# Another order for the first two batches of a packed attention and gated FFN kernel

## The chip, the cores and the metric

One NeuronCore of a Trainium2 chip runs the whole program. The metric is the device time of one execution in microseconds. The engines are TensorE (PE, matmuls and transposes; PEld is its weight load), VectorE (DVE), ScalarE (ACT), GpSimd (POOL) and SyncE (SP), which issues every DMA of this kernel.

## The reference, cut to what matters

```python
def _attn_ref(q, k, v, p):                    # q, k, v: 8 x 8 x 576 x 64, p: 8 x 8 x 32 x 64
    def sm_attn(qq, kk, vv):
        s = scale * np.matmul(qq, kk.transpose(0, 1, 3, 2))
        a = softmax(s)
        return np.matmul(a, vv)
    p_packed = sm_attn(p, k, v)               # softmax 1: 32 rows over 576 keys
    return sm_attn(q, p_packed, p_packed)     # softmax 2: 576 rows over 32 keys

x = attn_out.transpose(0, 2, 1, 3).reshape(4608, 512)
out = ((x @ w_a) * (x @ w_b)) @ w_out         # w_a, w_b: 512 x 1536, w_out: 1536 x 512
```

All inputs and the output are float32.

## The kernel before, in words

**Tiling.** The kernel goes batch by batch (8 batches of 576 tokens). For a batch, stage1 computes the packed attention for the even and the odd heads (e = 0, 1): scores on PE, maximum on DVE, exponential on ACT, transposes of the result on PE with copies on ACT, product with v on PE. stage2 computes the second attention as far as its probabilities: scores on PE, a transpose and a maximum on DVE, the difference (L328) on DVE or POOL, the exponential (L330) on ACT, sum and reciprocal on DVE, the product with the reciprocal (L337) on the engine of the difference, a transpose back on DVE (L341), a cast to the high part a_hi on ACT (L347) and the low part a_lo on DVE. The weights are not multiplied with x: g_tiles (L371) multiplies the packed values with a 256-column piece of w_a and of w_b, giving g, split into ghi (ACT, L377) and glo (DVE); mm1 (L389) multiplies g with the probabilities. The two factors come in two halves pa and pb; ACT copies pa to asb (L401), DVE multiplies pb into it (L404), which frees the two pairs of PSUM banks, and ACT and POOL split the result h into h_hi (L408) and h_lo. mm2 (L415, later L724) multiplies h with the split w_out. Every product of two split numbers is three matmuls: high by high, high by low, low by high.

**Weight words.** The weights arrive as raw 64-bit words in 36 pieces of 512 KB: piece 4c + n, for c = 0 to 5, holds a quarter of column block c of w_a (n = 0, 1) or w_b (n = 2, 3), and pieces 24 to 35 are rows of w_out. A piece takes three steps: A, its high words on ACT (high_word, L194); B, its low words on ACT (L202), DVE or POOL (both L199), as the digit of the piece in WAYS says (0 ACT, 1 DVE, 2 POOL); C, the join on DVE (both_words, L205). A C frees the piece's buffer, and SP may then load a further piece; 12 buffers exist. For w_out a step D follows, which splits the joined f32 tile on ACT and POOL; that tile, wo_f, has one buffer. A_i, B_i, C_i stand for the steps of piece i, counted from 0.

**The order.** The order on every engine and in SP's queue is the order of emission; nothing is moved by a scheduler. FIRST loads p, k, q, v of batch 0 and the first 11 pieces. START is the order of batch 0 up to its first product: T turns p, k0 to k4 and q0 to q4 turn the five parts of k and q (PE transposes, then copies on DVE or ACT by a digit of TURN, first five digits k, 0 DVE, 1 ACT), S0, r0 (e = 0) and S1, r1 (e = 1) are the next steps of stage1, P turns the packed values, s0 and s1 are the next steps of stage2, W is filler (nine matmuls without use, L562), g the first g_tiles, Lp, Lv, Lk, Lq are loads of the next batch. PLAN_0 is the order during batch 0: 37 slots divided by bars, two in each of the 12 mm1 (after pa and after pb), then one after each step of mm2; its steps S, r, s, T, P, k, q, L belong to batch 1. g_tiles for mm1 4 and 5 stands before mm1 3, and so on in pairs. PLAN is the same for batch 1, with steps of batch 2. From batch 2 on, 72 periods (period) follow STEPS, repeated every 24, and FILLS gives the number of mm2 matmuls between their products. SUBS gives the engine of L328 and L337 for batch 0, e = 0 and 1, and batch 1, e = 0 and 1 (0 POOL, 1 DVE); later batches use POOL.

**Loads.** Eight DMAs are out at a time: the issue of one waits until the eighth before it has landed. A half of k of a batch is four DMAs of 144 KB in 128-byte rows (L116), and is turned by one DVE transpose (L124).

Of the kernel before, what the change touches and what calls it, by code (L numbers as in the profile page):

```python
# [19 lines left out]
def tile_packed_attn_gated_ffn(  # L20
# [175 lines left out]
    def low_word(raw, way):  # L196
        low = raw[..., 0]
        if way:
            (nc.vector if way == 1 else nc.gpsimd).tensor_scalar(  # L199
                out=low, in0=low, scalar1=2.0 ** -29, scalar2=7.0, op0=ALU.mult, op1=ALU.min)  # L200
        else:
            nc.scalar.activation(out=low, in_=low, func=AF.Copy, scale=0.93 * 2.0 ** -29)  # L202
# [107 lines left out]
    def stage2(b, e):  # L310
# [17 lines left out]
        eng.tensor_tensor(out=s2, in0=s2, in1=mx.unsqueeze(2).broadcast_to([P, TU, J]), op=ALU.subtract)  # L328
# [180 lines left out]
    PLAN_0 = ("A | C C | B A B A | B C C B C | A A | C | B | C B A T0 k0 Lp2 A | A A B B C Lq0 | C C k1 | A B A | "
# [127 lines left out]
    for b in range(NB):  # L637
        plan = dict(PLAN if b else PLAN_0)
        slot, tasks, late_steps = [0], {"g": next_g(b + 1)} if b == 0 else {}, [""]

        def between():

            steps, _, late_steps[0] = plan.get(slot[0], "").partition(";")
            if b == 0:
                emit(1, steps, tasks)
            else:
                if 2 <= slot[0] and slot[0] % 4 == 0 and kept[0] < NC:
                    keep_weights()
# [307 lines left out]
```

## Time and profile before

| | us |
|---|---|
| median of the runs (lowest, highest) | 715.92 (714.87, 716.61) |
| profiled execution, its own time | 714.0 |
| its span | 712.2 |
| busy: PE, DVE, POOL, ACT | 699.0, 449.8, 417.8, 363.2 |
| start of the first product of batch 0 (L389) | 34.68 |
| filler W before it (L562) | 7.99 |

A row of the order in time gives start, duration, engine, line, operation, tile written and tiles read, shape, count of merged instructions, and in brackets the idle time before it with what ended it. In a row of windows come the stretch, its length, busy time and instructions of PE, PEld, DVE, ACT and POOL, the granted PE clock, the share of the DMA engines and GB/s.

### The profile page before, as it was taken

How to read it: one execution, taken by the hardware profiler on the slowest of the kernel's cores; microseconds unless marked ns; L12 is line 12 of the kernel's file. 1: busy time of each engine (PE TensorE's matmuls, PEld its weight loads, DVE VectorE, ACT ScalarE, POOL GpSimd, SP SyncE). 2: the span in 40 equal slices, each digit the busy share in tenths (PEclk: the TensorE clock that was granted, in tenths of full speed). 3: DMA queues.
4: the chain of work that ended last, by engine and by line, in shares of the span. 5: the costliest groups of instructions: out<-in, count | busy, mean ns of one | idle time of the engine just before them, and what ended most of it. 6: DMA issues, size and time to landing. Idle time of an engine off the chain costs nothing.

```text
span 712.2 us, 14198 instructions
## 1 busy us (share of the span) xinstructions
PE 699.0 (98%) x5558; PEld 574.2 (81%) x5558; DVE 449.8 (63%) x819; ACT 363.2 (51%) x733; POOL 417.8 (59%) x322
## 2 busy tenths in 40 slices
PE   6899999999999999999999999999999999999998
PEld 4488877888778887887888788788888888888887
DVE  3888755367455669665875668765785657754342
ACT  3788753554344455644563456554554455544520
POOL 0496753337334687745874579566776578856520
PEclk9999999999999999999999999999999999999999
DMA  8999872767344735555453574457146323133002
GB/s 230 387 274 315 220 162 53 193 153 282 93 98 139 211 96 141 139 138 146 134 111 115 142 195 93 106 176 182 61 98 180 105 89 119 61 110 127 1 1 74
DMA packets 177059, 102.37 MB, mean 144 GB/s; under 512 B 141280, under 2 KB 159456, under 8 KB 171616
## 3 DMA queue, kind: packets, MB, share of 16 engines
q1 hardware_dynamic: 176992, 101.47, 50.3%
q8 instruction: 43, 0.70, 0.4%
q14 instruction: 24, 0.20, 0.1%
HBM read 85.72 MB, written 15.73 MB: 142 GB/s over the span
## 4 chain that ended last, share of the span: by engine, by line
PE 94%; DVE 2%; SPq 1%; DMA 1%; ACT 1%; issue 0%; DVEq 0%; ACTq 0%
PE x L724 37%; PE m L765 29%; PE m L389 9%; PE x L779 5%; PE m L415 5%; PE s L301 2%; PE s L316 1%; PE s L255 1%; PE x L371 1%; PE s L291 1%; SPq L116 1%; DMA kn<-in_k_dram 1%; DMA nat<-in_k_dram 0%; PE m L152 0%; PE x L152 0%
## 5 line engine op out<-in xcount | busy, mean ns | idle before, releaser
L724 PE MATMUL x<-wo,h_hi 128*128 128x512 f32 (+1 forms) x776 | 249.3, 391 | 0.0
L91 POOL TENSOR_TENSOR h_lo<-asb,h_hi 128x576 fp32r<-128x576 f32 x96 | 140.3, 1462 | 83.3 <-ACT h_hi L810 44.6
L724 PEld LDWEIGHTS x<-wo,h_hi 128*128 128x128 f32 x776 | 140.8, 188 | 22.2 <-ACT gs L785 1.0
L724 PE MATMUL x<-wo,h_lo 128*128 128x512 f32 (+1 forms) x388 | 152.1, 392 | 0.0
L91 POOL TENSOR_TENSOR G_lo<-gs,G_hi 128x640 fp32r<-128x640 f32 x72 | 113.0, 1575 | 30.6 <-ACT G_hi L800 30.3
L724 PEld LDWEIGHTS x<-wo,h_lo 128*128 128x128 f32 x388 | 72.9, 188 | 11.8
L91 POOL TENSOR_TENSOR A_lo<-gs,A_hi 128x256 fp32r<-128x256 f32 x36 | 27.2, 754 | 89.7 <-ACT A_hi L788 89.7
L847 DVE TENSOR_TENSOR d<-m,d 128x576 f32<-128x576 f32 (+1 forms) x73 | 54.0, 740 | 34.6 <-ACT d L843 33.8
L860 DVE TENSOR_TENSOR asb<-m,d 128x288 f32<-128x288 f32 x72 | 32.4, 451 | 66.4 <-ACT c L856 64.8
L856 ACT COPY c<-m 128x288 f32<-128x288 f32 x72 | 28.8, 399 | 78.6 <-PE m L765 78.6
L734 DVE TENSOR_TENSOR part<-x,part 128x512 f32<-128x512 f32 (+1 forms) x65 | 44.1, 678 | 38.8 <-PE x L724 38.8
L765 PE MATMUL m<-tx_hi,G_hi 128*128 128x288 f32 x216 | 63.8, 296 | 0.0
L765 PE MATMUL m<-tx_hi,G_lo 128*128 128x288 f32 x216 | 63.7, 295 | 0.0
L785 ACT COPY gs<-x 128x512 f32<-128x512 f32 x36 | 21.1, 587 | 82.8 <-PE x L779 81.2
L765 PE MATMUL m<-tx_lo,G_hi 128*128 128x288 f32 x216 | 63.3, 293 | 0.0
L800 ACT CAST G_hi<-gs 128x640 fp32r<-128x640 f32 x72 | 52.2, 730 | 15.1 <-POOL gs L794 14.5
L843 ACT COPY d<-m 128x576 f32<-128x576 f32 (+1 forms) x73 | 46.6, 639 | 20.2 <-PE m L765 18.6
L810 ACT CAST h_hi<-asb 128x576 fp32r<-128x576 f32 x72 | 49.0, 680 | 11.5 <-DVE asb L874 11.5
L765 PEld LDWEIGHTS m<-a_hi,G_hi 128*128 128x128 f32 x144 | 27.0, 187 | 31.6 <-issue 17.4
L794 POOL TENSOR_TENSOR gs<-gs 128x512 f32<-128x512 f32 x36 | 46.7, 1296 | 2.6 <-DVE gs L791 2.5
L765 PE MATMUL m<-a_hi,G_hi 128*128 128x288 f32 x144 | 47.0, 326 | 0.0
L389 PE MATMUL m<-a_hi,ghi 128*128 128x288 f32 x192 | 43.2, 307 | 1.5 <-ACT ghi L377 1.5
(171 smaller groups left out, 1548.7 us busy)
## 6 DMA issues: line engine op xcount, KB each, us to landing
wr<-w_kept SPq DMA_DIRECT2D x36, 1024.0 KB
nat<-in_k_dram SPq DMA_DIRECT2D x56, 144.0 KB
nat<-in_q_dram SPq DMA_DIRECT2D x56, 144.0 KB
vt<-in_v_dram SPq DMA_DIRECT2D x28, 256.0 KB
out_dram<-part SPq DMA_DIRECT2D x27, 256.0 KB
raw<-in_moe_w_a_dram SPq DMA_DIRECT2D x12, 512.0 KB
raw<-in_moe_w_b_dram SPq DMA_DIRECT2D x12, 512.0 KB
raw<-in_moe_w_out_dram SPq DMA_DIRECT2D x12, 512.0 KB
```

What stands on the lines that cost most here:

```text
L91: return eng.tensor_tensor(out=dst, in0=src, in1=hi.bitcast(F32), op=ALU.subtract)
L389: nc.tensor.matmul(out=ps[:, half, 0:HS], lhsT=gt[:, kt, ft % 4, cols], rhs=at[:, kt, HS * half:HS * half + HS], start=(n == 0 and kt == 0 ...
L415: nc.tensor.matmul(out=o[:, cols], lhsT=ht[:, c0:c0 + P], rhs=wt[:, cols], start=(ft == 0 and n == 0), stop=(ft == NFT - 1 and n == 2))
L724: nc.tensor.matmul(out=o[:, cols], lhsT=ht[:, c0:c0 + P], rhs=wt[:, cols], start=(ft == fts[0] and n == 0), stop=end)
L734: nc.vector.tensor_tensor(out=parts[i][:, cols], in0=o[:, cols], in1=parts[i][:, cols], op=ALU.add)
L765: nc.tensor.matmul(out=bank[:, n % 2, 0:HS], lhsT=g, rhs=t, start=(first and i == 0), stop=(i == 2), skip_group_check=True)
L779: nc.tensor.matmul(out=gps[e][J * r:J * r + J, :], lhsT=ppT[rows, 2 * (b % 2), r, :], rhs=w[rows, r, :], start=True, stop=True)
L794: nc.gpsimd.tensor_tensor(out=gs[:, 2:4].rearrange("p a u f -> p a (u f)"), in0=gs[:, 0:2].rearrange("p a u f -> p a (u f)"), in1=s2.unsqu ...
L800: nc.scalar.copy(out=G_hi[:, n % 3], in_=gs[:, 1:6, n % 2])
L810: nc.scalar.copy(out=view(h_hi[ft]), in_=src)
L843: nc.scalar.copy(out=d[:, both], in_=X[:, both, 0:HS])
L847: nc.vector.tensor_tensor(out=d[:, both], in0=V[:, both, 0:HS], in1=d[:, both], op=ALU.add)
```

## The change

Nothing but constants changes: the order strings START, PLAN_0, PLAN, STEPS and FILLS, and the engine strings WAYS, TURN and SUBS. The instructions of PE are the same ones. On SP, in START, the load of p of batch 1 moves ahead of piece 13, pieces 18 and 19 move ahead of v and k of batch 1, and the two halves of k follow each other with pieces 20 and 21 behind them (before: v, first half, pieces 18 to 20, second half, piece 21).

```diff
-    START = ("T0 k0 k4 k1 k3 k2 q0 S0 S1 r0 r1 q1 r1 r0 r0 r1 r0 q2 r1 q3 q4 P0 s0 B s1 W A s0 B A A s0 s0 B s1 C "
-             "A s1 B s0 C s1 A s1 C B B Lp2 C A B A s0 s1 B C B B s0 B g A C A A s1 Lv2 Lk2 C C A A C B B Lk3 C s1")
-    WAYS = ("000000022220202120012012011200010010")
-    TURN = ("0001110101")
-    SUBS = ("0100")
+    START = ("T0 k0 k1 k3 k2 k4 q0 S0 r0 r1 r1 q1 r1 r0 r0 S1 A q3 r0 r1 B q2 B q4 P0 C s0 s0 s1 A B A s0 B Lp2 A A s0 s1 B s1 C B s1 A A W C s0 C A s1 C B s0 s1 C s0 g A B B A s1 B A C C s1 Lv2 B Lk2 Lk3 B C C B A")
+    WAYS = ("220000002222201201112002111221210002")
+    TURN = ("1111110000")
+    SUBS = ("0011")
...
-    PLAN_0 = ("A | C C | B A B A | B C C B C | A A | C | B | C B A T0 k0 Lp2 A | A A B B C Lq0 | C C k1 | A B A | "
-              "S0 B | B A r0 | C C C | B A Lq1 |  | C C B r0 r0 D A A | S1 C D | B C B B A D | r1 C | A A D | r0 T2 "
-              "|  | q0 B r1 C B D r1 C |  | A | D B C Lv1 A r1 | A B D Lk2 B C B q1 D Lk3 A A P0 | C s0 s0 D C Lp4 "
-              "A B | s1 s0 | Lv2 | D | s0 s1 s0 | k2 s0 s1 C k3 | s1 |  | Lq2 D s0 s1 s1 Lq3 s1")
+    PLAN_0 = ("A A | C C | A B | C B C A B | B A | C | C B | A A B B C T0 k0 Lp2 A | Lq0 C | B k1 C | A A B | C S0 C B | A r0 | B A C B C | A | | B C r0 Lq1 C r0 D A | C A D B S1 | A B C D | B r1 C r1 | A B D | r0 T2 | | C r1 A B D | C A | q0 C | Lv1 B r1 A D | B B Lk2 q1 Lk3 A D A C P0 B | A C s0 s0 C A Lp4 D | D s1 | Lv2 D | s0 s1 B s0 | C s0 | k2 s1 D s1 | s1 | s0 k3 s0 | Lq2 Lq3 s1 s1")
```

PLAN is rewritten in the same way, with the steps of batch 2 at most two slots from their old places. In STEPS single steps move by one place within a period or to the next one, for instance `11: {... 'h': 'Lq2', 'c': 'u2 G'}` to `11: {... 'h': 'G Lq2', 'c': 'u2'}`. In FILLS two entries change by one: `(5, 0, 5)` to `(5, 1, 4)` and `((5, 4, 4), (6, 5, 0))` to `((5, 3, 4), (7, 5, 0))`.

More of the change, by code (lines that the diff above doesn't have):

```diff
@@ L499, in tile_packed_attn_gated_ffn @@
     FIRST = ("p0 k0 k2 k1 q0 v0 q1 v1 q2 w1 w1 w1 w1 w1 w1 w1 w1 w1 w1 w1")
-    START = ("T0 k0 k4 k1 k3 k2 q0 S0 S1 r0 r1 q1 r1 r0 r0 r1 r0 q2 r1 q3 q4 P0 s0 B s1 W A s0 B A A s0 s0 B s1 C "
-             "A s1 B s0 C s1 A s1 C B B Lp2 C A B A s0 s1 B C B B s0 B g A C A A s1 Lv2 Lk2 C C A A C B B Lk3 C s1")
-    WAYS = ("000000022220202120012012011200010010")
-    TURN = ("0001110101")
-    SUBS = ("0100")
-    PLAN = (" |  |  | S0 | r0 | r0 |  | r0 |  | r0 Lv1 ; S1 | r1 | r1 q0 Lk2 | r1 | r1 | q1 Lk3 Lv2 P0 |  ; s0 | s0 s0 | s0 T2 | "
-            "s0 Lp4 | s0 s1 | s1 s1 | s1 | s1 | s1 | t0 t1 t2 t3 u0 | k2 |  | k3 Lq2")
+    START = ("T0 k0 k1 k3 k2 k4 q0 S0 r0 r1 r1 q1 r1 r0 r0 S1 A q3 r0 r1 B q2 B q4 P0 C s0 s0 s1 A B A s0 B Lp2 A A s0 s1 B s1 C B s1 A A W C s0 C A s1 C B s0 s1 C s0 g A B B A s1 B A C C s1 Lv2 B Lk2 Lk3 B C C B A")
+    WAYS = ("220000002222201201112002111221210002")
+    TURN = ("1111110000")
+    SUBS = ("0011")
+    PLAN = ("| | | S0 | r0 | | r0 | r0 | | r0 ; Lv1 S1 | r1 r1 | q0 Lk2 | r1 | r1 q1 Lk3 | Lv2 P0 | ; s0 | s0 s0 | T2 Lp4 | s1 | | s1 s1 s0 | | s1 s0 s1 | s0 k2 s1 | t0 u0 t1 k3 | | | t2 Lq2 t3")
     PLAN = dict(enumerate(PLAN.split("|")))
-    PLAN_0 = ("A | C C | B A B A | B C C B C | A A | C | B | C B A T0 k0 Lp2 A | A A B B C Lq0 | C C k1 | A B A | "
[3 rows of a table removed]
+    PLAN_0 = ("A A | C C | A B | C B C A B | B A | C | C B | A A B B C T0 k0 Lp2 A | Lq0 C | B k1 C | A A B | C S0 C B | A r0 | B A C B C | A | | B C r0 Lq1 C r0 D A | C A D B S1 | A B C D | B r1 C r1 | A B D | r0 T2 | | C r1 A B D | C A | q0 C | Lv1 B r1 A D | B B Lk2 q1 Lk3 A D A C P0 B | A C s0 s0 C A Lp4 D | D s1 | Lv2 D | s0 s1 B s0 | C s0 | k2 s1 D s1 | s1 | s0 k3 s0 | Lq2 Lq3 s1 s1")
     PLAN_0 = dict(enumerate(PLAN_0.split("|")))
@@ L892, in tile_packed_attn_gated_ffn @@
         between()
-    STEPS = {-2: {'post': 'u1 u2', 'd': 'G', 'h': 'H', 'b': 'u3'}, -1: {'post': 'H', 'h': 'G'}, 0: {'pre': 'S0', 'a': 'r0', 'c': 'H Lq1', 'w': 'G Lv1', 'end': 'r0'}, 1: {'pre': 'G', 'a': 'H', 'b': 'r0 r0', 'w': 'r0'}, 2: {'post': 'S1 H', 'h': 'r1', 'c': 'G'}, 3: {'pre': 'G', 'd': 'r1', 'a': 'r1', 'b': 'r1 H', 'f': 'q0', 'end': 'r1'}, 4: {'v': 'H', 'h': 'G', 'b': 'Lk2'}, 5: {'pre': 'P0 q1', 'd': 'G', 'v': 'T2', 'end': 's0 H'}, 6: {'pre': 'Lv2', 'post': 'Lk3 Lp4', 'v': 'H', 'a': 's0', 'b': 'G', 'c': 's0'}, 7: {'pre': 's0', 'post': 'H', 'a': 's0 G', 'c': 's0', 'end': 's0'}, 8: {'pre': 's1', 'post': 's1', 'd': 'H', 'a': 's1', 'c': 'G s1'}, 9: {'pre': 'k2', 'post': 'G', 'd': 's1', 'a': 'H', 'h': 's1', 'f': 's1', 'end': 't0'}, 10: {'v': 't1 t2 t3', 'a': 'u0', 'b': 'G', 'end': 'H'}, 11: {'post': 'u1', 'v': 'H', 'a': 'k3', 'h': 'Lq2', 'c': 'u2 G', 'f': 'u3'}, 12: {'pre': 'S0', 'b': 'Lq1', 'w': 'G', 'f': 'Lv1', 'end': 'H'}, 13: {'pre': 'G r0', 'd': 'r0', 'v': 'H', 'h': 'r0', 'b': 'r0', 'w': 'r0'}, 14: {'post': 'S1', 'a': 'H', 'b': 'G'}, 15: {'pre': 'G', 'post': 'H r1', 'd': 'r1', 'a': 'r1', 'h': 'r1', 'f': 'q0', 'end': 'r1'}, 16: {'v': 'G', 'h': 'H', 'b': 'Lk2', 'end': 'P0 q1'}, 17: {'pre': 'G', 'a': 'T2', 'b': 'H', 'end': 's0'}, 18: {'post': 'Lv2 s0 Lk3', 'v': 'G', 'h': 'Lp4', 'b': 's0', 'c': 'H', 'f': 's0'}, 19: {'pre': 'G', 'post': 's0', 'b': 's0', 'end': 'H s0'}, 20: {'pre': 's1', 'd': 's1', 'a': 's1 H', 'c': 's1', 'w': 'G'}, 21: {'pre': 'k2 G', 'v': 's1', 'a': 'H', 'w': 's1', 'f': 's1', 'end': 't0 t1'}, 22: {'pre': 't2', 'v': 'u0 H', 'h': 'G'}, 23: {'pre': 'u1', 'v': 'G t3', 'a': 'H', 'h': 'k3', 'c': 'Lq2 u2', 'end': 'u3'}}
@@ new lines, in tile_packed_attn_gated_ffn @@
+    STEPS = {-2: {'post': 'u1 u2', 'd': 'G', 'h': 'H', 'b': 'u3'}, -1: {'h': 'H G'}, 0: {'pre': 'S0', 'a': 'H', 'c': 'Lq1', 'w': 'Lv1 r0', 'f': 'G'}, 1: {'pre': 'G', 'v': 'r0', 'a': 'H', 'b': 'r0 r0', 'w': 'r0'}, 2: {'post': 'S1 H', 'b': 'r1', 'c': 'G'}, 3: {'pre': 'G', 'd': 'r1', 'a': 'r1', 'h': 'H', 'b': 'r1', 'f': 'q0', 'end': 'r1'}, 4: {'pre': 'H', 'h': 'G', 'b': 'Lk2', 'c': 'P0'}, 5: {'post': 'G', 'd': 'q1', 'v': 'T2', 'end': 's0 H'}, 6: {'pre': 'Lv2', 'post': 'Lk3 Lp4', 'v': 'H', 'a': 's0', 'b': 'G', 'c': 's0'}, 7: {'pre': 's0', 'post': 'H', 'a': 's0 G', 'w': 's0', 'end': 's0'}, 8: {'pre': 's1', 'post': 's1', 'd': 'H', 'a': 's1', 'c': 'G s1'}, 9: {'pre': 'k2', 'post': 'G', 'd': 's1', 'a': 'H', 'h': 's1', 'f': 's1', 'end': 't0'}, 10: {'post': 't1', 'v': 't2 t3', 'a': 'u0', 'b': 'G', 'end': 'H'}, 11: {'post': 'u1', 'v': 'H', 'a': 'k3', 'h': 'G Lq2', 'c': 'u2', 'f': 'u3'}, 12: {'pre': 'S0', 'b': 'Lq1', 'c': 'Lv1', 'w': 'G', 'end': 'H'}, 13: {'pre': 'G r0', 'v': 'H r0', 'h': 'r0', 'b': 'r0', 'w': 'r0'}, 14: {'post': 'S1', 'v': 'H', 'b': 'G'}, 15: {'pre': 'G', 'post': 'H r1', 'd': 'r1', 'a': 'r1', 'h': 'r1', 'f': 'q0'}, 16: {'pre': 'r1', 'v': 'G', 'h': 'H', 'b': 'Lk2', 'c': 'P0', 'end': 'q1'}, 17: {'pre': 'G', 'a': 'T2', 'b': 'H', 'w': 's0'}, 18: {'post': 'Lv2 s0 Lk3', 'v': 'G', 'a': 'H', 'b': 'Lp4', 'f': 's0 s0'}, 19: {'pre': 'G', 'post': 's0', 'c': 's0', 'end': 's1 H s0'}, 20: {'a': 's1 H', 'h': 's1', 'w': 'G', 'f': 's1'}, 21: {'pre': 'k2 G', 'd': 's1', 'a': 'H', 'w': 's1', 'f': 's1', 'end': 't0 t1'}, 22: {'pre': 't2', 'v': 'u0', 'a': 'H', 'h': 'G', 'end': 't3'}, 23: {'pre': 'u1', 'a': 'G', 'h': 'H k3', 'c': 'Lq2 u2', 'end': 'u3'}}
@@ L894, in tile_packed_attn_gated_ffn @@
     banks_of["x"], banks_of["v"] = bank_pair(), bank_pair()
-    FILLS = [((5, 2, 5), (5, 7, 0)), ((11, 1, 8), (9, 7, 0)), ((5, 0, 5), (6, 8, 0)), ((4, 3, 3), (6, 8, 0)), ((4, 4, 4), (5, 7, 0)), ((6, 3, 3), (7, 5, 0)), ((5, 3, 2), (9, 5, 0)), ((4, 4, 4), (5, 7, 0)), ((5, 4, 4), (6, 5, 0)), ((9, 7, 5), (10, 5, 0)), ((4, 4, 4), (5, 7, 0)), ((9, 4, 7), (8, 8, 0))]
+    FILLS = [((5, 2, 5), (5, 7, 0)), ((11, 1, 8), (9, 7, 0)), ((5, 1, 4), (6, 8, 0)), ((4, 3, 3), (6, 8, 0)), ((4, 4, 4), (5, 7, 0)), ((6, 3, 3), (7, 5, 0)), ((5, 3, 2), (9, 5, 0)), ((4, 4, 4), (5, 7, 0)), ((5, 3, 4), (7, 5, 0)), ((9, 7, 5), (10, 5, 0)), ((4, 4, 4), (5, 7, 0)), ((9, 4, 7), (8, 8, 0))]
```

## The prediction

> **What bounds the kernel now.** I read the page, then the chain of waits, then the rows of each engine in order of time for the first 70 us, the stretch that the change reorders.
>
> ```profile
> PE 699.0 (98%) x5558; PEld 574.2 (81%) x5558; DVE 449.8 (63%) x819; ACT 363.2 (51%) x733; POOL 417.8 (59%) x322
> PE 94%; DVE 2%; SPq 1%; DMA 1%; ACT 1%; issue 0%; DVEq 0%; ACTq 0%
> ```
>
> TensorE is busy for 699.0 of 712.2 us and carries 94% of the chain. The change adds no matmul and takes none away, so it can win only holes in PE's row, or lose by making new ones. PE's rows in order of time (start, duration, instruction, idle time before it and its releaser) show where holes are:
>
> ```profile
> 23.46 7.99 PE L562 MATMUL m<-kn,ident 128*128 128x512 f32 x18
> 31.63 1.57 PE L371 MATMUL x<-w_ab,ppT 64*32 64x512 f32 x16 [0.17 <-DVE w_ab L205]
> 34.68 0.54 PE L389 MATMUL m<-a_hi,ghi 128*128 128x288 f32 x2 [1.48 <-ACT ghi L377]
> 37.27 0.54 PE L389 MATMUL m<-a_lo,ghi 128*128 128x288 f32 x2 [0.26 <-DVE a_lo L91]
> 38.80 1.18 PE L371 MATMUL x<-w_ab,ppT 64*32 64x512 f32 x16
> 44.91 0.43 PE L389 MATMUL m<-a_hi,ghi 128*128 128x288 f32 x2
> 59.72 0.68 PE L255 MATMUL s<-xT,pT 64*32 64x288 f32 x12 [0.20 <-DVE xT L124]
> 68.08 0.43 PE L389 MATMUL m<-a_hi,ghi 128*128 128x288 f32 x2
> ```
>
> L562 is filler. The first useful product of batch 0 starts at 34.68, and from 38.80 PE has almost no hole. So the gain is how much earlier 34.68 comes, as far as nothing later makes PE wait again.
>
> **The change, part by part.** *What sets 34.68 now* is the chain through batch 0's second softmax, on ACT and DVE:
>
> ```profile
> 25.20 0.69 ACT L330 ACTIVATE s<-s 128x576 f32<-128x576 f32 x1 [1.20 <-POOL s L328]
> 27.48 0.67 ACT L330 ACTIVATE s<-s 128x576 f32<-128x576 f32 x1
> 34.05 1.07 ACT L377 CAST ghi<-x 128x512 fp32r<-128x512 f32 x2
> 25.93 0.78 DVE L328 TENSOR_TENSOR s<-s,mx 128x576 f32<-128x576 f32 x1
> 28.34 0.74 DVE L334 TENSOR_REDUCE sum<-s 128x18 f32<-128x576 f32 x1
> 29.81 1.08 DVE L337 TENSOR_TENSOR s<-s,sum 128x576 f32<-128x576 f32 x1
> 30.81 1.28 DVE L205 SCALAR_TENSOR_TENSOR w_ab<-raw 128x512 uint32<-128x512 uint32 x2
> 32.01 1.42 DVE L341 STREAM_TRANSPOSE a2f<-s 128x576 f32<-128x576 f32 x2
> 36.46 0.76 DVE L91 TENSOR_TENSOR a_lo<-a2f,a_hi 128x576 fp32r<-128x576 f32 x1
> 24.02 1.16 POOL L328 TENSOR_TENSOR s<-s,mx 128x576 f32<-128x576 f32 x1 [22.71 <-DVE mx L325]
> 28.03 1.41 POOL L337 TENSOR_TENSOR s<-s,sum 128x576 f32<-128x576 f32 x1 [2.86 <-DVE sum L336]
> ```
>
> Second exponential, sum, product with the reciprocal, two joins (L205), two transposes, two casts, then ghi at 34.05: all in line.
>
> *Turns of k and q.* The five k copies and q0 go to ACT, q1 to q4 to DVE.
>
> ```profile
> 11.98 0.69 DVE L154 COPY xT<-m 128x512 f32<-128x512 f32 x1 [1.01 <-PE m L152]
> 13.58 0.76 DVE L261 TENSOR_REDUCE nmx<-s 128x1 f32<-128x576 f32 x1 [0.91 <-PE s L255]
> ```
>
> Now k2's copy ends at 12.67 and the scores at 13.55. With k4's two short copies last on ACT, and no 0.69 after k2, the scores end some 0.35 earlier. That reaches the filler (23.46 becomes 23.1), but not the softmax, for the next reason.
>
> *Weight words on ACT.* In the new order ACT does the low words 2 to 5 and the high words up to 4 around the exponentials, and exp 0 stands behind A4, the high word of piece 4. When does piece 4 land? SP's queue shows it: only eight transfers are out at once, so the issue of piece 12 waits for piece 4.
>
> ```profile
> 24.14 0.42 SPq L215 DMA_DIRECT2D raw<-in_moe_w_b_dram  x1
> SPq L215 <- DMA raw<-in_moe_w_a_dram: 0.9, 1, 0.9
> 29.63 12.54 POOL L199 TENSOR_SCALAR raw<-raw 128x512 uint32<-128x512 uint32 x5 [0.19 <-DMA raw<-in_moe_w_b_dram]
> 60.70 0.68 ACT L194 ACTIVATE raw<-raw 128x512 f32<-128x512 f32 x1 [2.59 <-DMA raw<-in_moe_w_a_dram]
> 61.27 0.66 ACT L202 ACTIVATE raw<-raw 128x512 uint32<-128x512 uint32 x1
> 66.73 0.64 ACT L401 COPY asb<-m 128x576 f32<-128x576 f32 x1
> ```
>
> 24.14 + 0.42 + 0.9 = 25.46. Piece 7 lands at 29.63 (POOL waited for it), so a piece takes (29.63 - 25.46)/3 = 1.39. A4 takes 0.57 (two words start 0.57 apart, at 60.70 and 61.27), so exp 0 starts at 26.05, 0.85 *later* than now. B4, B5 and exp 0 itself, 0.57 to 0.6 each, put exp 1 at 27.8 (now 27.48). Sum and reciprocal (28.34 to 29.79 now) end at 29.75.
>
> *Softmax 2 of batch 0 wholly on POOL.* Its second difference hides: it takes 1.16 and can begin at 25.3 at the latest, when DVE has the second maximum today (the 25.93 row follows 0.6 of a join), and exp 1 starts at 27.8. The second product is on the path: 1.41 instead of 1.08, to 31.15. What pays for this is the order of DVE: the two joins, 1.28, no longer stand between product and transposes, since C2, C3 and C4 fit into DVE's waits for ACT and POOL. The first transpose is done before 31.0, the second runs 31.2 to 31.9 (now until 33.4); its cast ends at 32.5, the first ghi at 33.1. The other road, filler and g (23.1 + 7.99 + 1.1, from the 38.80 row), ends at 32.2 and is no later. So 34.68 becomes 33.1: -1.6. The low part a_lo of the second half, now 36.46, follows ghi's at 34.4, so the 0.26 at 37.27 goes too: PE leads by 1.85.
>
> [...]
>
> *Three places where PE may wait again.* The lead that is left is the least that any of them lets through. Their rows, POOL, SP, DVE, and windows whose last two columns are the DMA share and GB/s:
>
> ```profile
> 55.45 2.02 POOL L199 TENSOR_SCALAR raw<-raw 128x512 uint32<-128x512 uint32 x1 [1.27 <-DMA raw<-in_moe_w_a_dram]
> 40.88 6.74 SPq L116 DMA_DIRECT2D nat<-in_k_dram  x4
> 49.45 6.36 SPq L116 DMA_DIRECT2D nat<-in_k_dram  x4
> 58.28 1.38 DVE L124 STREAM_TRANSPOSE xT<-nat 128x1152 f32<-128x1152 f32 x1 [1.02 <-DMA nat<-in_k_dram]
> 44.00:48.80 4.80, 4.80 (x46) 3.80 (x45) 4.14 (x8) 4.40 (x9) 4.64 (x3) 1.00 0.95 127
> 50.00:54.00 4.00, 4.00 (x33) 4.00 (x32) 2.85 (x5) 2.81 (x6) 2.91 (x3) 1.00 1.05 379
> 55.00:56.00 1.00, 1.00 (x20) 0.55 (x5) 1.00 (x3) 1.00 (x3) 0.55 (x1) 1.00 0.37 59
> ```
>
> (a) POOL's low words. B8 to B12 stand on POOL, and POOL begins them at 31.15 instead of 29.63. C11 needs the fourth; behind C11 in DVE's queue are two glo (0.6 each) and the product that frees the bank of the next half, in all 2.5. At 2.51 each (12.54/5) that ends at 43.7, at the 2.02 of the 55.45 row at 41.7. PE wants that bank at 44.91 - 1.85 = 43.06. Loss 0 to 0.65; I take 0.4, nearer the first, since DVE is as full as now. Lead 1.45. A queue that is early gains nothing.
>
> (b) k of batch 1. Now the order on SP is k's first half, pieces 18 to 20, k's second half; PE waits 0.20 for it at 59.72. In the new order pieces 18 and 19 go first, then v, both halves of k (127 GB/s, words 379), then piece 20. One piece fewer is ahead of k: 1.39 earlier, and the slow gap that now lies between the halves goes. So PE's S0 may come 1.4 to 2 earlier: no bound on 1.45. The lower end is in the rivals.
>
> (c) Pieces 20 to 23. The bytes up to piece 21 are the same in both orders. Now ACT waits 2.59 for that piece's high word, at 60.70, and works from there without a gap to the copy at 66.73, which at 67.37 frees the bank that PE takes at 68.08: 0.7 to spare. In the new order B22 (now DVE) is one more word on ACT in that row: 0.57. So with piece 21 as late as now the lead that passes is 0.15. The piece lands earlier by what DMA wastes less: in the window from 55 to 56, after a k load, it moves 59 GB/s, 0.84 us lost against 379, and such a gap comes once instead of twice. I take 0.85, between 0 and 1.6 (both gaps gone). Lead that passes: 1.0, between 0.15 and the 1.45 that (a) leaves.
>
> *The rest.* Batch 1's difference and product go to DVE (SUBS): four instructions of 0.78 or 1.08, off the path as long as the last a_lo is ready.
>
> ```profile
> 120.46 0.76 DVE L91 TENSOR_TENSOR a_lo<-t,a_hi 128x576 fp32r<-128x576 f32 x1 [0.74 <-ACT a_hi L347]
> 122.74 0.42 PE L389 MATMUL m<-a_hi,ghi 128*128 128x288 f32 x2
> ```
>
> It is ready 1.5 before PE's row; in the new order half 0 is finished a slot earlier and only transposes, cast and a_lo of half 1 are left for the last slot, so this cover grows. Fourteen low words on POOL instead of ten, later in slots where no bank hangs on them: nothing, between -0.3 and +0.5. PLAN, STEPS and FILLS move single steps by one place in stages where PE has no hole: nothing, between -0.5 and +0.5.
>
> Sum: -1.6 - 0.25 + 0.4 + 0.45 = -1.0. The profiled execution took 714.0 (span 712.2 and 1.8 around it), 1.9 under the median of 715.92; a shift of the span carries over, so 715.9 - 1.0 = 714.9.
>
> **The rivals.**
> *The whole lead passes.* If piece 21 lands 1.6 earlier and POOL's words run at 2.02, nothing holds PE: -1.85, 714.1. For it: PE's rows have no other hole. Against: in the windows of words and of k DMA's share is 1.05 and 0.95, so little of it can be won.
>
> *The start does not move.* If piece 4 lands later than 25.46, or ACT's words slip behind each other, exp 0 takes the lead back one for one; 1.9 later, nothing is left of it: 715.9. For it: three waits for DMA are put into ACT's order ahead of exp 0.
>
> *Slower: k comes late.* SP's two k rows take 6.74 and 6.36, 13.1 together. From the end of the second (55.81) to the end of xT (59.66) it is 3.85. If the pace stays and SP can begin k only at t, xT ends at t + 16.95; slower by 1.43 or more when t is past 44.1. Pieces 18 and 19 and v stand ahead, and SP waits for the transfer eight before, piece 16, which at 1.39 a piece lands at 42.1 or, with p between, a little after. Begun at 45.5, xT ends at 62.45 and PE loses 2.8: 718.7. Against: SP's pace may be that of a queue which is full of words. Counted in bytes, the words and v are through at 46.8 (44.0, where the 127 GB/s begin, and two pieces), and both halves (1.18 MB) at 127 GB/s take 9.3, to 56.1; with the turn, and for landing at most the 2.47 from SP's last issue to DVE's start, xT ends between 57.5 and 59.95.
> [...]
>
> **How the numbers follow.** 0.2%, 1.43 us, is about what a measurement of this kernel tells from no change. Within it: the forecast (0.34) and the start that does not move (0.12), 0.46. Faster: the whole lead, with or without half a microsecond from the later stages, 0.37. Slower: k late 0.10, or DVE standing behind joins C30 to C33, which the new order puts ahead of the splits that free their one buffer, 0.07. For the likeliest case alone, 714.3 to 715.9. Eight in ten: from 715.9 - 1.85 - 0.5 and 0.6 for the medians (single runs of before lie from 714.87 to 716.61), 713.0, to half-way into the late k, 717.3.
>
> **What would show it.** Right: PE's first L389 near 33.1 with ACT as releaser; exp 0 starting at 26 behind a word; no 0.26 behind a_lo; PE's L389 after the fourth g (68.08) only about 1 earlier, waiting for ACT's copy of asb. Wrong: exp 0 before 25.5 or after 27; L255 of batch 1 waiting more than 0.5 for xT; a hole at 43 larger than 0.7; new holes after 120.

## The result, and the profile after

| | before | after |
|---|---|---|
| median of 20 runs each, us (lowest, highest) | 715.19 (713.38, 716.70) | 716.79 (715.60, 718.74) |
| profiled execution, us; its span | 714.0; 712.2 | 718.01; 716.0 |

The ratio is 1.0028 (95% interval 1.0019 to 1.0037): slower by some 2 us (the medians lie 1.6 apart). 716.79 lies inside the range that I gave, but not where I forecast it: I had said 1.0 faster, 714.9, and 0.17 for slower. The two profiled executions lie 4.0 apart, the ratio says 2.0; so the rows below show the places, and the ratios the sizes.

The page's lines on busy time and on the chain, of after:

```profile
PE 698.8 (98%) x5558; PEld 574.4 (80%) x5558; DVE 454.9 (64%) x823; ACT 360.3 (50%) x727; POOL 424.0 (59%) x324
PE 88%; DMA 4%; DVE 3%; POOL 1%; issue 1%; ACT 1%; SPq 1%; DVEq 0%; ACTq 0%; POOLq 0%
```

PE is busy for as long as before (698.8 against 699.0) and carries 88% of the chain instead of 94%: in the span, what was added is waiting. PE's rows in order of time, of after, the same instructions as those shown of before and the two that are new:

```profile
31.66 1.09 PE L371 MATMUL x<-w_ab,ppT 64*32 64x512 f32 x16
34.92 0.54 PE L389 MATMUL m<-a_hi,ghi 128*128 128x288 f32 x2 [2.17 <-ACT ghi L377]
38.21 0.68 PE L389 MATMUL m<-a_lo,ghi 128*128 128x288 f32 x2
39.92 1.09 PE L371 MATMUL x<-w_ab,ppT 64*32 64x512 f32 x16
45.84 0.44 PE L389 MATMUL m<-a_hi,ghi 128*128 128x288 f32 x2
59.83 0.72 PE L255 MATMUL s<-xT,pT 64*32 64x288 f32 x24
68.34 0.43 PE L389 MATMUL m<-a_hi,ghi 128*128 128x288 f32 x2
79.78 0.54 PE L389 MATMUL m<-a_hi,ghi 128*128 128x288 f32 x2 [1.85 <-ACT asb L401]
86.48 0.53 PE L389 MATMUL m<-a_hi,ghi 128*128 128x288 f32 x2 [0.26 <-DVE asb L404]
```

Three things are to be seen. The first product starts at 34.92: no earlier. The next g comes at 39.92, where it was 38.80, though the hole of 0.26 behind a_lo is gone: the pairs in between take 0.68 instead of 0.43. And 1.85 us of waiting stand at 79.78, in a stretch where PE had no hole before, with 0.26 more at 86.48. Between 59.83 and 68.34 PE is only 0.1 to 0.3 late. Some 0.6 more go at 69.5 in this one profile, behind a wait of DVE of 1.22 for piece 24 at 66.80; no other run's profile has that loss.

### The profile page after: what moved, and what is told of

Same layout as the page of the kernel before. It is cut to its first block, busy times and chain, and to the rows that moved or that the text cites. A ratio compares the mean times of both kernels' runs of the same rounds, so it can differ in the third digit from the quotient of the medians.

```text
span 716.0 us, 14203 instructions
## 1 busy us (share of the span) xinstructions
PE 698.8 (98%) x5558; PEld 574.4 (80%) x5558; DVE 454.9 (64%) x823; ACT 360.3 (50%) x727; POOL 424.0 (59%) x324
## 4 chain that ended last, share of the span: by engine, by line
PE 88%; DMA 4%; DVE 3%; POOL 1%; issue 1%; ACT 1%; SPq 1%; DVEq 0%; ACTq 0%; POOLq 0%
PE x L719 36%; PE m L760 29%; PE m L389 7%; PE m L415 5%; PE x L774 5%; PE s L301 1%; DMA raw<-in_moe_w_out_dram 1%; PE s L316 1%; DMA vt<-in_v_dram 1%; PE s L255 1%; DVE w_ab L205 1%; DMA raw<-in_moe_w_a_dram 1%; PE s L291 1%; DMA wr<-w_kept 1%; PE x L371 1%
## 5 line engine op out<-in xcount | busy, mean ns | idle before, releaser
L729 DVE TENSOR_TENSOR part<-x,part 128x512 f32<-128x512 f32 (+1 forms) x65 | 44.1, 679 | 38.2 <-PE x L719 38.1
L389 PE MATMUL m<-a_hi,ghi 128*128 128x288 f32 x192 | 44.0, 311 | 4.3 <-ACT ghi L377 2.2
```

The lines of the kernel that those rows point to most:

```text
L389: nc.tensor.matmul(out=ps[:, half, 0:HS], lhsT=gt[:, kt, ft % 4, cols], rhs=at[:, kt, HS * half:HS * half + HS], start=(n == 0 and kt == 0 ...
L729: nc.vector.tensor_tensor(out=parts[i][:, cols], in0=o[:, cols], in1=parts[i][:, cols], op=ALU.add)
```

## The experiments

Each was timed against the kernel before on the same chip; a ratio is to before, with its 95% interval. "Gate 1" and "gate 2" are the holes near 79 and near 86.

### Which part of the change loses: the start, PLAN_0, or the later stages

```diff
 e1_start:  START, TURN, WAYS[:13], SUBS[:2] new, the rest old
 e2_plan0:  PLAN_0, WAYS[13:], SUBS[2:] new, the rest old
 e3_late:   PLAN, STEPS, FILLS new, the rest old
 e4_b24, on the changed kernel (a low word to ACT, one slot later):
-  slot 13 "B A C B C", slot 14 "A",   WAYS[24] = 1
+  slot 13 "B A C C",   slot 14 "B A", WAYS[24] = 0
```

> The old kernel with the new start alone: START, TURN, the low words of pieces 0 to 12 and the engine of batch 0's softmax 2. Theory 1 (the time is lost in slots 13 to 17 of batch 0, where DVE waits for piece 24): within 0.5 us of before, PE's first L389 within 0.5 of 34.7 and mm1 of ft 6 within 0.5 of 60.4. Theory 2 (the start loses it: PE stands 2.2 us before its first L389 and then runs 5 us at a granted clock of 0.66): 1.5 to 2 us slower than before, with a granted clock below 0.8 between 35 and 40.

> The old kernel with the new order of batch 0's slots alone: PLAN_0, the low words of pieces 13 to 35, and batch 1's softmax 2 on DVE. Theory 1: 2 to 3 us slower than before (0.3 to 0.4%), with a wait of PE of more than 1 us for ACT's asb between 75 and 82, and DVE waiting for piece 24 near 66. Theory 2: within 0.5 us of before.

> The old kernel with the new PLAN, STEPS and FILLS alone (batch 1 and the periods). Both theories: within 0.5 us of before; a third, that the late stages lose it, would show 1.5 us or more here.

> The changed kernel with one low word moved: piece 24 is done on ACT in slot 14 instead of on DVE in slot 13 ahead of the join of piece 22. Theory 1: 2 to 2.7 us faster than the changed kernel, so 714.1 to 714.8 against a before of 715.2 (ratio 0.998 to 1.000), and no wait of PE for asb near 79. Theory 2: as slow as the changed kernel (ratio 1.002 to 1.003).

| | ratio |
|---|---|
| e1_start | 1.0013 (1.0004 to 1.0021) |
| e2_plan0 | 1.0046 (1.0034 to 1.0058) |
| e3_late | 1.0001 (0.9991 to 1.0011) |
| e4_b24 | 1.0034 (1.0022 to 1.0046) |

The later stages cost nothing, as forecast. The start alone loses a little instead of gaining, and the order during batch 0 loses by itself no less than the whole change. e4 took away DVE's wait for the piece and gained nothing. Where the start alone loses its 0.13% stays open: its one profile (714.3) is the fastest of its runs (median 715.75). PE's rows of e1 (first row) and e2 (second):

```profile
60.35 0.54 PE L389 MATMUL m<-a_hi,ghi 128*128 128x288 f32 x2 [0.47 <-ACT asb L401]
79.54 0.54 PE L389 MATMUL m<-a_hi,ghi 128*128 128x288 f32 x2 [1.49 <-ACT asb L401]
```

In e1 PE waits for ACT's copy, as in (c) but at an earlier product, and from there to the end of batch 0's mm1 its rows are those of before; in e2 gate 1 stands with the old start too.

### What makes gate 1

First the chain behind 79.78 in after, read from rows of DVE, POOL and ACT in order of time:

```profile
71.88 1.66 DVE L205 SCALAR_TENSOR_TENSOR wo_f<-raw 128x512 uint32<-128x512 uint32 x1
71.56 1.43 POOL L91 TENSOR_TENSOR h_lo<-asb,h_hi 128x576 fp32r<-128x576 f32 x1 [1.85 <-ACT h_hi L408]
73.58 0.62 ACT L230 CAST wo<-wo_f 128x512 fp32r<-128x512 f32 x1 [0.92 <-DVE wo_f L205]
74.33 1.29 POOL L91 TENSOR_TENSOR wo<-wo_f,wo 128x512 fp32r<-128x512 f32 x1 [1.34 <-issue]
75.58 1.43 POOL L91 TENSOR_TENSOR h_lo<-asb,h_hi 128x576 fp32r<-128x576 f32 x1
75.66 1.91 DVE L205 SCALAR_TENSOR_TENSOR wo_f<-raw 128x512 uint32<-128x512 uint32 x1 [1.45 <-POOL wo L91]
77.60 0.62 ACT L230 CAST wo<-wo_f 128x512 fp32r<-128x512 f32 x1 [1.68 <-DVE wo_f L205]
78.12 1.07 ACT L377 CAST ghi<-x 128x512 fp32r<-128x512 f32 x2
79.08 0.65 ACT L401 COPY asb<-m 128x576 f32<-128x576 f32 x1
```

C24, the first join into the one buffer of wo_f; D0 on ACT and POOL; C25, which needs that buffer; D1 on ACT; behind it in ACT's queue ghi and the copy that frees PE's bank. Before, the same steps (DVE, POOL, DVE, ACT) were:

```profile
69.62 0.69 DVE L205 SCALAR_TENSOR_TENSOR wo_f<-raw 128x512 uint32<-128x512 uint32 x1
69.90 1.70 POOL L91 TENSOR_TENSOR h_lo<-asb,h_hi 128x576 fp32r<-128x576 f32 x1 [1.12 <-ACT h_hi L408]
73.19 0.69 DVE L205 SCALAR_TENSOR_TENSOR wo_f<-raw 128x512 uint32<-128x512 uint32 x1 [0.34 <-POOL wo L91]
73.92 0.62 ACT L230 CAST wo<-wo_f 128x512 fp32r<-128x512 f32 x1 [0.36 <-DVE wo_f L205]
```

These two joins take 0.69 there and 1.66 and 1.91 in after. The two long ones begin 0.32 and 0.08 behind the start of an h_lo on POOL and end 0.55 and 0.56 behind its end (71.56 + 1.43 = 72.99, and 71.88 + 1.66 = 73.54). Before, the join began 0.28 ahead of h_lo, and it was h_lo that took 1.70 instead of 1.43: in these rows the one that began second took longer, by 0.27 to 1.22.

```diff
 e5_d1, on the changed kernel (D1 behind ghi in ACT's queue):
-  slot 17 "C A D B S1", slot 18 "A B C D"
+  slot 17 "C A B S1",   slot 18 "A B D C D"
 e6_start_w10:  e1_start with warm(n=10)
 e7_d1_w10:     e5_d1 with warm(n=10)
 e8_mix:  START, TURN, WAYS[:24], SUBS[:2], slots 0 to 12 new, warm(n=10),
          slot 13 "B A C C", slots 14 to 36 and all else old
```

> The changed kernel with the split D1 moved from slot 17 to slot 18, behind the ghi of ft 10 and the copy of pa of ft 9 in ACT's order. Theory A (PE's 1.85 us wait near 79 is ACT standing at D1 for a join of DVE that itself waits for POOL): that wait goes and the kernel is 1.5 to 2.7 us faster than the changed one, ratio to before 0.999 to 1.001. Theory B (DVE and POOL are late as a whole there, whatever ACT's order): no faster than the changed kernel, ratio 1.002 to 1.004, with the wait near 79 or the next one longer.

> The new start alone with ten filler matmuls instead of nine, which shortens PE's standstill before its first L389 from 2.0 to about 1.1 us. Theory A (a standstill of 2 us lowers the granted clock for the next 3 to 5 us): the clock stays at 1.0 between 35 and 40, the fourth g (L371 near 46.6) comes 1 to 1.7 us earlier, and the kernel takes 0 to 1 us less than the new start alone, ratio to before 0.999 to 1.0005; what it does not win is taken by the wait of PE for ACT near 60. Theory B (the low clock has another cause): clock 0.66 as before and the same time, ratio 1.001.

> The changed kernel with both edits, D1 behind ghi and ten filler matmuls. If both reasons hold, the gains add up as far as the words let them: 2 to 3.5 us faster than the changed kernel, ratio to before 0.998 to 1.000. If only D1's place counts, as the kernel with D1 moved; if only the clock, within 1 us of the changed kernel.

> A version meant to be better than both: the new start with ten fillers, the new slots 0 to 12 of batch 0, where piece 20 is wanted later, the old slots from 14 on with their low words, batch 1's softmax 2 on POOL, PLAN, STEPS and FILLS old. If the words of pieces 20 to 23 are the next limit: 0.5 to 1.5 us faster than before, ratio 0.998 to 0.9995, PE's g near 63.7 about 1 us earlier than before. If the new slots 0 to 12 carry part of the loss of the new order: slower than before by 0.5 us or more.

| | ratio | clock, 35 to 40 |
|---|---|---|
| e5_d1 | 1.0043 (1.0030 to 1.0055) | 0.72 |
| e6_start_w10 | 1.0025 (1.0009 to 1.0041) | 1.00 |
| e7_d1_w10 | 1.0038 (1.0025 to 1.0052) | 1.00 |
| e8_mix | 1.0001 (0.9990 to 1.0012) | 1.00 |

Moving D1 moved the wait. POOL takes low word 27 before its part of D1, the next join C26 stands until 81.00, and the product behind it in DVE's queue comes late (POOL, POOL, DVE, PE of e5):

```profile
77.28 2.34 POOL L199 TENSOR_SCALAR raw<-raw 128x512 uint32<-128x512 uint32 x1
79.70 1.27 POOL L91 TENSOR_TENSOR wo<-wo_f,wo 128x512 fp32r<-128x512 f32 x1
81.00 0.69 DVE L205 SCALAR_TENSOR_TENSOR wo_f<-raw 128x512 uint32<-128x512 uint32 x1 [1.25 <-POOL wo L91]
82.41 0.54 PE L389 MATMUL m<-a_hi,ghi 128*128 128x288 f32 x2 [2.08 <-DVE asb L404]
```

A tenth filler keeps the clock, but by itself brings no time: in e6 PE then waits at 50.24 for DVE's product, which stands behind a join that waited for a word of POOL, and in e8 PE is 0.9 early at the third g (45.70 against 46.60), 0.34 at the fifth (63.42 against 63.76), and waits 0.54 at 78.96. The old order has gate 1 as well, closed just enough to take a lead: before, DVE's product there (77.72, taking 0.74) ends less than 0.1 ahead of PE's row at 78.53 that needs its bank. e8 shows that with slots 14 to 36 of old nothing is lost.

```profile
50.24 0.54 PE L389 MATMUL m<-a_hi,ghi 128*128 128x288 f32 x2 [0.77 <-DVE asb L404]
78.96 0.53 PE L389 MATMUL m<-a_hi,ghi 128*128 128x288 f32 x2 [0.54 <-DVE asb L404]
```

### Two gates in a row

```diff
 e9_c25, on the changed kernel (C25 alone into an idle buffer of batch 1's work tiles):
-  t = sm.tile([P, DO], F32, name="wo_f32", bufs=1)
+  t = wk.tile([P, S], F32, name="t1", bufs=2)[:, 0:DO] if n == 1 else sm.tile(... "wo_f32", bufs=1)
 e10_new19:  e8_mix with slots 19 to 36, WAYS[28:] and SUBS new
 e11_new16:  e8_mix with slots 16 to 18 new, slot 19 "B r1 C"
 e12_three:  e9_c25 with e4's edit and warm(n=10)
```

> Changed kernel, but the joined word of piece 25 goes into the idle second buffer of batch 1's work tiles, not into the one buffer of wo_f, so that C25 no longer waits for POOL's part of D0. Theory 1 (the chain C24, D0, C25, D1, ghi, asb is what costs PE its 1.85 us at 79.78): C25 runs right behind the product at 73.5 and ends between 74.8 and 76.2 (the later end if POOL's part of D0 has begun first and holds it), PE's wait for ACT's asb near 79.8 shrinks to 0.5 or less, and the time falls by 1.0 to 1.8: ratio to the kernel before 1.0005 to 1.0015 instead of 1.0028. Theory 2 (PE is late for another reason, and this wait only shows it): the wait goes but PE waits as long within the next 15 us, ratio 1.002 or more.

> The mixed order that came out equal to the kernel before (new start, new slots 0 to 12, ten fillers), with the new order of slots 19 to 36, the new engines for low words from piece 28 on and batch 1's softmax on DVE. Theory 1 (slots 16 to 18 carry the loss): 0.9990 to 1.0012, no new wait of PE behind 80. Theory 2 (POOL's added words 28, 30 and 35, or batch 1's softmax, carry it): 1.002 to 1.004.

> The mixed order that came out equal to the kernel before, with the new order of slots 16 to 19 alone (piece 25's low word ahead of the joins 23 and 24, one high word fewer ahead of D1). Theory 1 (slots 16 to 18 carry the loss by C24, D0, C25, D1): PE waits 1 to 2 us for ACT's asb near 79 to 80, ratio 1.0015 to 1.0030. Theory 2 (later slots): within 0.9990 to 1.0010.

> Changed kernel with three repairs at once: ten fillers (granted clock 1.00 between 35 and 40), piece 24's low word on ACT a slot later, and a buffer of its own for piece 25's joined word. Theory 1 (clock loss of 1.3 at the start, and C24, D0, C25, D1 in the middle, are the whole loss): no wait of PE above 0.6 between 70 and 90, ratio 0.9985 to 1.0005. Theory 2 (something else in slots 13 to 36 costs): 1.002 or more.

| | ratio | hole near 79 | hole near 86 |
|---|---|---|---|
| e9_c25 | 1.0030 (1.0017 to 1.0044) | none | 1.28 |
| e10_new19 | 1.0051 (1.0035 to 1.0068) | 0.53 | 2.10 |
| e11_new16 | 1.0023 (1.0013 to 1.0032) | 1.13 | none |
| e12_three | 1.0014 (1.0003 to 1.0024) | none | 1.26 |

My theory of one chain fell with e9: the wait for ACT's asb went, as it should, and a wait for DVE's product took its place 5 us later (PE of e9):

```profile
84.69 0.54 PE L389 MATMUL m<-a_hi,ghi 128*128 128x288 f32 x2 [1.28 <-DVE asb L404]
```

And both halves of the order lose by themselves: slots 16 to 18 at gate 1 (e11), as much as I had expected of them, and slots from 19 on at gate 2 (e10), where I had expected no wait. Gate 2 in e10 (POOL, POOL, DVE, DVE, DVE, PE, and the window from 85 to 90):

```profile
77.80 4.15 POOL L199 TENSOR_SCALAR raw<-raw 128x512 uint32<-128x512 uint32 x2
82.03 1.28 POOL L91 TENSOR_TENSOR wo<-wo_f,wo 128x512 fp32r<-128x512 f32 x1
83.35 1.88 DVE L205 SCALAR_TENSOR_TENSOR wo_f<-raw 128x512 uint32<-128x512 uint32 x1 [2.77 <-POOL wo L91]
85.41 0.41 DVE L199 TENSOR_SCALAR raw<-raw 128x512 uint32<-128x512 uint32 x1
85.73 0.75 DVE L404 TENSOR_TENSOR asb<-m,asb 128x576 f32<-128x576 f32 x1
86.54 0.53 PE L389 MATMUL m<-a_hi,ghi 128*128 128x288 f32 x2 [2.10 <-DVE asb L404]
85.00:90.00 5.00, 3.46 (x18) 3.40 (x19) 2.98 (x10) 1.85 (x4) 2.69 (x2) 0.74 0.86 242
```

POOL's words stand ahead of its part of D2, that part releases the buffer for C27, C27 meets an h_lo (1.88; before it did so too, 1.90, but began at 80.02), and between C27 and the product now stand batch 1's reciprocal and low word 29, both new there. In after the same C27 reads:

```profile
83.06 1.90 DVE L205 SCALAR_TENSOR_TENSOR wo_f<-raw 128x512 uint32<-128x512 uint32 x1 [0.70 <-POOL wo L91]
```

PE comes late to it there, from gate 1, and waits only 0.26. The hole of 2.10 in e10 also costs clock: 0.74 in the window from 85 to 90.

Three things were left to settle: whether the two gates are the whole of it, what the clock is worth, and whether the lead then passes.

```diff
 e13_gate2, on the changed kernel (gate 2 alone):
-  slot 19 "B r1 C r1", slot 23 "C r1 A B D",    WAYS[27:30] = 2, 2, 1
+  slot 19 "B r1 C",    slot 23 "r1 C r1 A B D", WAYS[27:30] = 0, 0, 0
 e14_both:  e13_gate2 with e9's buffer
 e15_all:   e14_both with e4's edit and warm(n=10)
 e16_mix2:  e8_mix with e9's buffer and WAYS[27] = 0
```

> Changed kernel with the second gate alone mended: low words 27 to 29 on ACT (27 and 28 were POOL's, 29 DVE's), and the reciprocal of batch 1's second sum back in slot 23. Two gates in series: PE's wait of 1.85 for ACT's asb near 79.8 stays, the one near 86 goes, ratio 1.0015 to 1.0030. Rival (the words on POOL and DVE are the cause by themselves): 0.9990 to 1.0010.

> Changed kernel with both gates mended: a buffer of its own for C25, low words 27 to 29 on ACT, the reciprocal back in slot 23. Two gates in series: no wait of PE above 0.5 between 75 and 90, and what is left is the start's clock loss of about 1.3 against its lead: ratio 0.9995 to 1.0012. Rival (a further gate behind 90, or the load of the moved words on ACT): 1.002 or more.

> As the run before, and ten fillers (clock) and piece 24's low word on ACT a slot later. Two gates and the clock are the whole loss: granted clock 1.00 between 35 and 40, no wait of PE above 0.5 between 75 and 90, ratio 0.9980 to 1.0003. Rival: 1.001 or more.

> The mixed order that came out equal to the kernel before (new start, new slots 0 to 12, ten fillers, old slots 14 to 36), with a buffer of its own for C25 and low word 27 on ACT. If the old order's slots 16 to 18 are the same gate, only less far closed (PE waited 0.54 at 78.96 there), the wait goes and the lead of 0.3 that PE has at 63.4 passes: 0.9985 to 1.0000, the fastest of all. Rival (a gate behind it takes the lead as well): 0.9998 to 1.0012.

| | gate 1 stays | gate 1 mended |
|---|---|---|
| gate 2 stays | after: 1.0028 (1.0019 to 1.0037) | e9: 1.0030 (1.0017 to 1.0044) |
| gate 2 mended | e13: 1.0044 (1.0031 to 1.0057) | e14: 1.0014 (1.0001 to 1.0027) |
| both, and clock and piece 24 | | e15: 0.9999 (0.9990 to 1.0009) |

Either gate alone brings nothing, both together some 0.14% (the intervals overlap a little), and with the clock and piece 24 the changed kernel comes out equal to before: from after to e15 it is 0.29%, with intervals well apart. The two steps between can each be read twice, within 0.01%: with gate 1 mended, mending gate 2 is worth 0.16% (e9 to e14) and 0.15% (e12 to e15), the clock with piece 24 0.16% (e9 to e12) and 0.15% (e14 to e15). Single steps of that size are hardly clear of their intervals, and e9 and e12 ran on another chip than e14 and e15. e16, at 1.0007 (0.9998 to 1.0016), is no faster: in its profile the first product came at 35.82, so there was no lead to pass, and whether one would pass stays open. PE's row of e13, and then lines of the view of waits of e15 (in all, times, longest), where neither hole is left; its last 0.2 lies at 54.03:

```profile
79.20 0.54 PE L389 MATMUL m<-a_hi,ghi 128*128 128x288 f32 x2 [1.48 <-ACT asb L401]
```

```profile
...
PE m L389 <- ACT ghi L377: 1.2, 1, 1.2
PE s L316 <- DVE ppT L243: 0.5, 1, 0.5
PE m L760 <- DVE a_lo L91: 0.4, 1, 0.4
PE m L760 <- DVE asb L869: 0.3, 1, 0.3
PE m L389 <- DVE asb L404: 0.2, 1, 0.2
...
```

Open is the size of e13: its one profile shows gate 1 only, and a shorter gate than after's, yet it is slower than I had expected. The share of piece 24's word in the step from e14 to e15 was not tried apart from the clock.

## Why the prediction was wrong, by its own steps

The sum was 1.85 of lead, less 0.85 of losses at three places, and nothing for the rest. Two of these terms failed: the lead, which did not come, and the rest, which was not nothing but about 1.1 us (0.14 to 0.16%). The clock, about as much again together with piece 24's word, was not in the sum.

*The start, -1.85: it did not move.* That was a rival (0.12). Seven kernels have the new START with nine fillers: their first L389 starts between 33.83 (e1) and 35.94 (e5), 35.04 in the mean; three have the old one: 34.68 to 35.12, mean 34.84. In e1 and after, exp 0 did stand behind piece 4's word as I had put it (ACT of e1, twice ACT of after, and twice DVE of after):

```profile
25.87 0.67 ACT L330 ACTIVATE s<-s 128x576 f32<-128x576 f32 x1
26.96 0.67 ACT L330 ACTIVATE s<-s 128x576 f32<-128x576 f32 x1
23.67 0.68 ACT L202 ACTIVATE raw<-raw 128x512 uint32<-128x512 uint32 x1 [1.36 <-DMA raw<-in_moe_w_b_dram]
29.34 0.63 DVE L205 SCALAR_TENSOR_TENSOR w_ab<-raw 128x512 uint32<-128x512 uint32 x1
29.88 0.74 DVE L334 TENSOR_REDUCE sum<-s 128x18 f32<-128x576 f32 x1
```

26.05 was near e1; in after the words came later (the third row is a wait for one), and ACT's order hands every such delay on. The second miss is the sentence that the joins fit into DVE's waits: from exp 1 to the first product I had 5.3, measured are 6.27 in after (28.65 to 34.92), since a join of 0.63 stands ahead of the second sum (the last two rows) and sum, product and transposes all follow it. In eleven of the fifteen kernels with the new START, with nine or ten fillers, exp 0 waits for POOL's first difference instead of a word, and from exp 1 to the first product it is 7.2, as long as before. There (DVE and POOL of e5) the first sum stands behind two joins:

```profile
27.02 2.25 DVE L205 SCALAR_TENSOR_TENSOR w_ab<-raw 128x512 uint32<-128x512 uint32 x2
27.18 1.54 POOL L328 TENSOR_TENSOR s<-s,mx 128x576 f32<-128x576 f32 x1 [0.31 <-DVE mx L325]
```

Before, two joins took 1.28. Of these two the second alone takes 1.65 and ends 0.55 behind POOL's second difference, so the first sum starts 1.6 after exp 0 has ended. All fifteen have this long join (1.64 to 1.67), also after and e1, where exp 0 is late and it costs less. I had written that the second difference on POOL hides; it does so for ACT, but not for the join on DVE. No run was made without it.

*The clock: not in the sum at all.* Windows of one and two us, of after:

```profile
33.00:35.00 2.00, 0.08 (x1) 0.08 (x1) 2.00 (x4) 1.53 (x4) 1.95 (x1) 1.00 0.93 333
35.00:36.00 1.00, 1.00 (x5) 0.86 (x6) 1.00 (x2) 1.00 (x3) 0.97 (x1) 0.71 0.92 276
37.00:38.00 1.00, 1.00 (x6) 1.00 (x6) 1.00 (x2) 1.00 (x3) 0.92 (x2) 0.50 1.02 343
39.00:40.00 1.00, 1.00 (x16) 0.83 (x22) 0.72 (x2) 0.77 (x2) 0.92 (x2) 1.00 1.03 358
```

I had priced PE's standstill between g and the first product at its length. It grew from 1.48 to 2.17, and the granted clock fell to 0.50 behind it. From the first product to the next g it is 5.00 instead of 4.12, with a hole of 0.26 fewer: 1.1 lost. At S0 of batch 1 only 0.1 of it is left (59.83 against 59.72), because before PE waited there for xT; and keeping the clock alone gained nothing (e1 to e6, e5 to e7).

*(a), POOL's words: right in kind, the place wrong.* No run waits at the product that I had named (44.91 before); e8 carries 0.9 of lead past it. e6, with the clock kept, waits 0.77 some 5 us later, at 50.24, where DVE's join waited 0.83 for POOL's next word; I took 0.4 and had 0.65 as the end.

*(b), k: right.* S0 of batch 1 ran in one piece at 59.83 with no wait, and the slower rival on k fell: SP began k at 44.82, past the 44.1 that I had named, but took 9.80 for both halves, not 13.1, and the last turn ended at 58.82, within my 57.5 to 59.95.

*(c), ACT's words up to the copy: right in kind.* e1 waits 0.47 for ACT's asb at 60.35, an earlier copy than the one at 66.73 that I had named.

*"The rest": the step that made the kernel slower.* Batch 1's softmax on DVE, POOL's fourteen words and the order behind slot 13 stood at nothing, between -0.3 and +0.5. My reason was that no bank hangs on those words. It does: word 27 on POOL stands ahead of D2, D2 frees wo_f for C27, and DVE's product, which frees PE's bank, stands behind C27; C24, D0, C25 and D1 hang together in the same way. I had followed SP's queue and the words' landing, but no chain through that single buffer. Batch 1's softmax on DVE and POOL's words 30 and 35 are in e15 too, which comes out equal to before, so there they cost nothing that shows. Gate 1 shows as 1.85 in the profile, and mending both gates gives back 0.14%. My rival on DVE standing behind joins (0.07) named this one buffer, but put the loss at C30 to C33. And none of the signs that I had named for being wrong came (the largest new hole after 120 is 0.2): the new holes stand at 79 and 86, where I had listed no place.

*The parts do not add.* The start (+0.13%) and PLAN_0 (+0.46%) make +0.28% together. That would fit gates in a row, at which PE's lateness is free because they open by other engines' work; no run was made for it, so it is not shown.

## What to carry to other kernels

When a reordering is priced, list every buffer with one copy and follow its chain of producer, consumer and next producer through each engine's queue, as far as the instruction in one of those queues that frees a bank for PE: words without a bank of their own stood on the path here. Where mending one wait gains nothing, look a few us later for the next one before dropping the theory, and mend both together: e9 and e13 alone would have cleared both gates of blame. A standstill of PE before a dense stretch is to be priced with the granted clock behind it (0.50 behind 2.17 us in after), though a later wait may give that loss back, as at S0 here. An operation that moves to POOL is to be looked at beside DVE's joins of the same moment (1.64 to 1.67 beside the second difference here; before, two joins took 1.28).

## What was not expected of the hardware

Ahead of the first product, standstills that differ little part the runs: behind 1.08 to 1.48 us (before, e2, e3, e6, e7, e8, e10, e11, e12, e15, e16) the granted clock stayed at 1.00, behind 1.91 (e9) to 2.19 us (after, e1, e4, e5, e9, e13, e14) it fell, to 0.50 for about 3.4 us in the windows of after. The length of the standstill alone does not settle it: behind 2.08 us at 82.41 in e5 and 2.09 at 81.51 in e7 the clock stayed at 1.00, behind 2.10 at 86.54 in e10 it fell. What else does is not shown.

A join on DVE was slow beside a split on POOL: begun 0.01 to 0.98 us behind the split, it took 1.00 to 1.95 instead of 0.63 to 0.69 and ended 0.54 to 0.56 behind the split's end (rows of before, after and ten of the experiments). In e8 the two starts lay under 0.02 us apart (69.58 and 69.57), and the join took 1.95. Beside POOL's difference at the start a join took 1.64 to 1.67.
